# Delta-rule attention and a low-rank mixer: channel products placed one instruction at a time

## Chip, cores and metric

The kernel runs on one core of a Trainium2 chip. Times are device microseconds of one execution on that core. The kernel before took 682.71 us, the median of 13 runs between 678.31 and 686.07.

## What is computed

All data is fp32. There are 4 batches of 8 heads, 768 tokens and head dimension 48; the heads side by side make 384 channels, and the mixer's inner width is 1536. Cut to what matters:

```python
# attention: a 48x48 state per batch and head, token after token
k_n = k / (norm(k) + 1e-6)
for t in range(S):
    y[t]  = q[t] @ state
    state = state + beta[t] * outer(k_n[t], v[t] - k_n[t] @ state)
# bridge: (B, H, S, D) -> x of shape (B, S, H*D)
h  = x.transpose(0, 2, 1) @ U @ V          # mixes tokens, rank 32
u  = x + h.transpose(0, 2, 1)
out = u + relu(u @ w_ch1) @ w_ch2          # the two channel products
```

## The kernel before, in words

**Attention** works in chunks of 64 tokens, 12 to a batch, and in halves of 6 chunks, numbered n = 0 to 7 (two to a batch). For each half the keys, queries and values are loaded (`load_keys`, `load`, `load_queries`), the keys' norms and gates are made (`norms`), and `grams` turns keys and queries on TensorE (`turn`, line 506) and forms their small products (`products`, line 520), two chunks at a time, so three pairs for keys and three for queries. `blocks` inverts the 32-token triangular blocks on VectorE, by 31 pairs of operations (lines 651 and 657), moves them through a scratch in DRAM, and joins them on TensorE (lines 705 and 719). `recur` (line 849) then goes through the 12 chunks in order. A chunk is: a product with the state (`from_state`, line 853), a subtraction on VectorE (line 883, tile rhs), a product (line 890), a copy on ScalarE (line 899, tile z), two more sets of products (lines 904 and 912), the new state on VectorE (line 927), and two copies of the output to the token tile on ScalarE (line 934). All its matmuls are small, with 48 or 64 rows and 64 columns of the array.

**The mixer** works on half a batch, 384 tokens, at a time. `front` (line 941) makes the low-rank token mixing (lines 954 and 968), adds it on VectorE, and turns the result (line 976). `wide` (line 987) makes the two channel products. The first, lines 1004 to 1016, goes over 12 slices f of the inner width; each slice is three matmuls 128x128 by 384 into one PSUM tile p_f, then a relu on ScalarE into h_f. The second, lines 1020 to 1037, goes over three blocks of 128 tokens; each accumulates 12 matmuls into a tile p_o, which VectorE adds to x and SyncE stores. Over the whole kernel these are 288 matmuls of each kind.

**The order of the work** is written by a small planner in the kernel itself, lines 104 to 179, before anything runs; the chip's engines then follow the written order. Each of the functions above is a Python generator. It yields `need(...)`, a list of results that must have been written, and `step(...)`, which says what the instructions up to the next yield cost on each engine in estimated microseconds, which PSUM tiles they take and give back, and how long afterwards (`then`) the next step can start. `run` (line 138) keeps an estimated clock for each engine. It picks again and again the step that could start earliest; on a tie, the part with the lower place comes first. Places are given at lines 1041 to 1056: recurrences of batches 1 to 3 have 5.01 to 5.03, grams from 2.1 to 5.5, `front` 1.5, `relu`, `store` and the blocks of `front` 1, and `wide` 6 to 9.5. A part with a place under 5 that becomes ready within 0.4 of a chosen step's own time on the same engine goes ahead of it (lines 160 to 165). Batches meet in three places: `front` needs the recurrence of its own batch, `recur(b)` needs batch b - 2 to be mixed (line 863), and the loads of a half need the recurrence of an earlier one.

PSUM is shared by tags, each with two slots: "pair" (two banks each) for the recurrence and later grams, "one" for turns, norms and `front`, "mix" for the channel products, early grams and early joins. A step that takes a tag is not picked while the planner counts no free slot of it.

The step that matters here, in the first channel product, covers three matmuls at an estimated 1.95 us:

```python
            yield step(pe=1.95, take=("mix",))
            p_f = ps_mix([128, GT], "p_f")
            for t in range(KT):
                nc.tensor.matmul(
```

Of the kernel before, what the change touches and what calls it, by code (L numbers as in the profile page):

```python
# [19 lines left out]
GT = 384  # L20
# [5 lines left out]
def kernel(  # L26
# [31 lines left out]
    DM = H * D  # L58
# [16 lines left out]
    mix = ctx.enter_context(tc.tile_pool(name="mix", bufs=2))  # L75
# [7 lines left out]
    def ps_pair(name):  # L83

        t = psum.tile([128, 2, 512], FP32, name=name, tag="pair", bufs=2)
        return t

    def ps_tile(shape, name, tag):
        t = psum.tile([128, 512], FP32, name=name, tag=tag, bufs=2)
        dims = "abcd"[: len(shape) - 1]  # L90
        return t[0 : shape[0], 0 : math.prod(shape[1:])].rearrange(
            f"p ({' '.join(dims)}) -> p {' '.join(dims)}", **dict(zip(dims, shape[1:]))
        )

    def ps_one(shape, name):
        return ps_tile(shape, name, "one")

    def ps_mix(shape, name):
        return ps_tile(shape, name, "mix")
# [9 lines left out]
    def need(*keys):  # L109

        return [k for k in keys if all(x >= 0 for x in k[1:])]

    def step(pe=0, dve=0, act=0, sp=0, pool=0, then=0.0, on=None, take=(), give=()):

        return dict(
            pe=pe, dve=dve, act=act, sp=sp, pool=pool, then=then, on=on, take=take, give=give
        )

    def emitted(key, after=0.0):
        done[key] = clock["now"] + after
# [9 lines left out]
    def begin(part, place):  # L132

        i = (place, len(parts))
        parts[i], waits[i] = part, []
        advance(i, clock["now"])
# [130 lines left out]
    def w1_there(f):  # L267
        return "weights", 1 + KT * (f * 128 // WIDE + 1)

    def w2_there(f):  # L270
        return "weights", 2 + KT * DFF // WIDE + f // 2
# [74 lines left out]
    def half(i, size=L):  # L346
        return slice(L * i, L * i + size)
# [151 lines left out]
    def grams(n, place):  # L499


        yield need(("k", n), ("room", n), ("pg", 0 if n == 1 else -1))
        kn = keys[n]
        kq, pg, qk = made[n]

        def turn(ts, places):

            p_t = ps_one([128, 2, 2, 2 * L], "p_t")
            yield step(pe=0.45, then=0.1, take=("one",))
            for x, (t, c) in enumerate(ts):  # L510
                for j in range(2):
                    nc.tensor.transpose(  # L512
                        p_t[:, x, j],
                        t[:, c, 2 * j : 2 * j + 2].rearrange("p s d -> p (s d)"),
                        ident,
                    )
            yield step(act=0.6, then=0.1, give=("one",))
            nc.scalar.copy(places, p_t)  # L518

        def products(c0, i):  # L520

            banks = ("mix", "mix") if n < 3 - i else ("pair",)
            yield step(pe=0.8, then=0.1, take=banks)
            if len(banks) == 2:
                p_g = [ps_mix([128, 512], "p_g") for _ in range(2)]
            else:
                t = ps_pair("p_g")
                p_g = [t[:, par] for par in range(2)]
            p_g = [t[:, 0:256].rearrange("p (c j t) -> p c j t", c=2, j=2) for t in p_g]
            for c in range(2):  # L530
                for j in range(2):
                    for par, x in QUADS:
                        rows, cols = half(par, D), half(x)

                        to = half(1 - x) if par == 1 and i == 0 else cols
                        nc.tensor.matmul(  # L536
                            p_g[par][to, c, j],
                            kq[rows, c0 + c, j, 0, cols],
                            kq[rows, c0 + c, j, i, cols],
                            start=True,  # L540
                            stop=True,
                        )
            at = slice(c0, c0 + 2)
            if i == 0:
                yield step(**{"dve" if n == 0 else "act": 0.7}, give=banks)
                copy = nc.vector.tensor_copy if n == 0 else nc.scalar.copy
                for par in range(2):
                    copy(pg[:, at, par], p_g[par])
            else:
                yield step(dve=0.9, give=banks)  # L550
                for par in range(2):
                    nc.vector.tensor_tensor(  # L552
                        out=qk[:, at, par],
                        in0=p_g[par],
                        in1=mask_u[:, None, None, :].to_broadcast([128, 2, 2, L]),
                        op=ALU.mult,
                    )

        def key_pair(c0):
            if n > 2 and c0 + 2 > UC // 2:  # L560
                yield need(("ksq", n))
            yield from turn([(kn, c0), (kn, c0 + 1)], kq[:, c0 : c0 + 2, :, 0])
            emitted(("keys turned", n, c0 // 2))
            yield from products(c0, 0)
            emitted(("p", n, c0 // 2), 0.5)

        def query_pair(c0):
            yield need(("q", n), ("p", n, c0 // 2))
            yield from turn([(qt, c0), (qt, c0 + 1)], kq[:, c0 : c0 + 2, :, 1])
            yield from products(c0, 1)  # L570
            emitted(("g", n, c0 // 2), 0.5)

        qt = qns[n == 1]
        key_place, query_place = place
        for c0 in range(0, UC, 2):
            begin(key_pair(c0), key_place + 0.001 * c0)
        yield need(*[("p", n, i) for i in range(UC // 2)])
        emitted(("pg", n))
        for c0 in range(0, UC, 2):
            begin(query_pair(c0), query_place + 0.001 * c0)  # L580
        yield need(*[("g", n, i) for i in range(UC // 2)])
        emitted(("grams", n))
        emitted(("turned", n))
# [403 lines left out]
    def wide(b, i):  # L987
        yield need(("front", b, i), ("narrow", b - (i == 0), 1 - i))
        x, ut, hs = xs[b], uts[b, i], {}

        def relu(f, p_f):
            yield step(act=0.5, then=0.1, give=("mix",))
            hs[f] = mix.tile([128, GT], FP32, name="h_f", bufs=12)
            nc.scalar.activation(hs[f], p_f, ACTF.Relu)  # L994
            emitted(("h", b, i, f))

        def store(c, p_o):
            yield step(dve=0.57, sp=0.4, give=("mix",))
            nc.vector.tensor_tensor(out=x[:, c], in0=x[:, c], in1=p_o, op=ALU.add)  # L999
            nc.sync.dma_start(out=out[b, c * 128 : (c + 1) * 128, :], in_=x[:, c])  # L1000
            if c + 1 == NB:
                emitted(("mixed", b))

        for f in range(FT):
            yield need(w1_there(f))
            yield step(pe=1.95, take=("mix",))
            p_f = ps_mix([128, GT], "p_f")
            for t in range(KT):
                nc.tensor.matmul(  # L1009
                    p_f,  # L1010
                    w1_sb[:, t, f * 128 : (f + 1) * 128],
                    ut[:, t],
                    start=(t == 0),
                    stop=(t == KT - 1),
                )
            begin(relu(f, p_f), 1)
        emitted(("wide", b, i))
        first = i * GT // 128

        for cs in [(0, 1), (2,)] if (b, i) == (0, 0) else [(0,), (1,), (2,)]:  # L1020
            p_os = {}
            for f in range(0, FT, 3):
                for c in cs:
                    yield need(w2_there(f + 2), ("h", b, i, f + 2))
                    yield step(pe=1.95, take=("mix",) if f == 0 else ())
                    if f == 0:
                        p_os[c] = ps_mix([128, DM], "p_o")
                    for e in range(f, f + 3):
                        nc.tensor.matmul(  # L1029
                            p_os[c],  # L1030
                            hs[e][:, c * 128 : c * 128 + 128],
                            w2_sb[:, e],
                            start=(e == 0),
                            stop=(e == FT - 1),
                        )
            for c in cs:
                begin(store(first + c, p_os[c]), 1)
        emitted(("narrow", b, i))
# [16 lines left out]
    for b in range(B):  # L1055
        order += [(wide(b, 0), 6 + b), (wide(b, 1), 6.5 + b)]
# [35 lines left out]
```

## Time and profile before

| what | before |
|---|---|
| median of 13 runs | 682.71 us |
| profiled execution, own time | 680.38 us |
| its span | 678.7 us |
| TensorE matmul busy | 630.3 us, 93% |
| VectorE busy | 316.5 us, 47% |
| ScalarE busy | 200.7 us, 30% |
| GpSimd busy | 42.6 us, 6% |
| first channel product (line 1009) | 203.9 us, 576 records of 498 ns |
| second channel product (line 1029) | 200.8 us, 576 records of 495 ns |
| mean DMA rate | 68 GB/s |

A page of the profile tells of one execution. Busy times are the union of an engine's records. An fp32 matmul leaves two records. Matmuls are pipelined, so records overlap, and the distance from one start to the next says more than the length of a record. A group's line gives the source line, engine, operation, output and inputs, shape, count, busy time and mean length, then the idle time of the engine ahead of it and what ended most of that. The granted TensorE clock is 1.00 from 140 us to the end, apart from one stretch at 0.91 and the last at 0.97, and lower before that.

### The profile page before, as it was taken

How to read it: one execution, taken by the hardware profiler on the slowest of the kernel's cores; microseconds unless marked ns; L12 is line 12 of the kernel's file. 1: busy time of each engine (PE TensorE's matmuls, PEld its weight loads, DVE VectorE, ACT ScalarE, POOL GpSimd, SP SyncE). 2: the span in 40 equal slices, each digit the busy share in tenths (PEclk: the TensorE clock that was granted, in tenths of full speed). 3: DMA queues.
4: the chain of work that ended last, by engine and by line, in shares of the span. 5: the costliest groups of instructions: out<-in, count | busy, mean ns of one | idle time of the engine just before them, and what ended most of it. 6: DMA issues, size and time to landing. Idle time of an engine off the chain costs nothing.

```text
span 678.7 us, 19659 instructions
## 1 busy us (share of the span) xinstructions
PE 630.3 (93%) x8668; PEld 403.4 (59%) x8668; DVE 316.5 (47%) x791; ACT 200.7 (30%) x487; POOL 42.6 (6%) x80
## 2 busy tenths in 40 slices
PE   5538899689999999999999999999999999999997
PEld 4438788556555665566556654655655555555554
DVE  6666777888794228736812594377111011000000
ACT  2405566343411531243214323403221220120210
POOL 6451000100000000000000000000000000000000
PEclk9855755699999999998999999999999999999999
DMA  8586738736513322262033404110200000000000
GB/s 123 111 198 129 165 111 205 176 67 120 143 31 72 76 49 48 69 108 61 2 81 77 95 2 94 38 47 26 37 14 25 2 0 24 12 1 23 12 10 26
DMA packets 143892, 46.00 MB, mean 68 GB/s; under 512 B 136960, under 2 KB 140032, under 8 KB 143808
## 3 DMA queue, kind: packets, MB, share of 16 engines
q1 hardware_dynamic: 133952, 30.99, 22.8%
q0 software_dynamic: 3552, 12.88, 6.7%
q10 hardware_dynamic: 6304, 0.89, 0.8%
q8 instruction: 68, 1.11, 0.7%
q14 instruction: 16, 0.13, 0.1%
HBM read 33.62 MB, written 11.11 MB: 66 GB/s over the span
## 4 chain that ended last, share of the span: by engine, by line
PE 77%; DVE 10%; DMA 7%; ACT 2%; issue 2%; SPq 2%; ACTq 1%; DVEq 0%
PE p_f L1009 27%; PE p_o L1029 26%; PE p_g L536 4%; PE p_y L853 3%; PE p_t L512 3%; PE p_h L968 3%; DVE prod L651 2%; PE p_s L904 2%; DVE xt L657 2%; PE p_s L890 2%; DMA zt<-scr 2%; PE p_y L912 2%; DMA scr<-xt 1%; PE p_e L777 1%; PE p_u L976 1%
## 5 line engine op out<-in xcount | busy, mean ns | idle before, releaser
L1009 PE MATMUL p_f<-ut,w_sb 128*128 128x384 f32 x576 | 203.9, 498 | 0.2 <-ACT h_f L994 0.2
L1029 PE MATMUL p_o<-w_sb,h_f 128*128 128x384 f32 x576 | 200.8, 495 | 0.2 <-DVE x L999 0.2
L1029 PEld LDWEIGHTS p_o<-w_sb,h_f 128*128 128x128 f32 x576 | 104.8, 190 | 64.5 <-DVE x L999 0.4
L1009 PEld LDWEIGHTS p_f<-ut,w_sb 128*128 128x128 f32 x576 | 104.7, 191 | 63.9 <-issue 1.5
L994 ACT ACTIVATE h_f<-p_f 128x384 f32<-128x384 f32 x96 | 47.1, 491 | 200.9 <-PE p_f L1009 200.8
L657 DVE TENSOR_TENSOR xt<-xt,prod 96x112 f32<-96x112 f32 (+21 forms) x216 | 70.5, 326 | 7.4
L651 DVE TENSOR_TENSOR prod<-gs,xt 96x112 f32<-96x112 f32 (+21 forms) x216 | 70.0, 324 | 5.9
L999 DVE TENSOR_TENSOR x<-x,p_o 128x384 f32<-128x384 f32 x24 | 13.2, 552 | 125.4 <-PE p_o L1029 125.4
L536 PE MATMUL p_g<-kq 48*64 48x64 f32 x1536 | 41.0, 254 | 11.4 <-DVE qk L552 8.1
L927 DVE TENSOR_TENSOR s<-s,p_s 128x192 f32<-128x192 f32 x40 | 14.1, 352 | 69.7 <-PE p_s L904 68.6
L536 PEld LDWEIGHTS p_g<-kq 48*64 48x64 f32 x1536 | 34.7, 162 | 19.6 <-DVE qk L552 7.6
L934 ACT COPY x<-p_y 64x192 f32<-64x192 f32 x96 | 30.1, 314 | 47.6 <-PE p_y L912 41.9
L853 PEld LDWEIGHTS p_y<-s,kq 48*64 48x64 f32 x1408 | 28.7, 153 | 20.1 <-issue 12.9
L853 PE MATMUL p_y<-s,kq 48*64 48x48 f32 x1408 | 34.2, 241 | 1.4 <-DVE prod L651 1.1
L883 DVE TENSOR_TENSOR rhs<-vn,p_y 128x192 f32<-128x192 f32 x44 | 15.5, 353 | 42.7 <-PE p_y L853 42.3
L899 ACT COPY z<-p_s 128x192 f32<-128x192 f32 x48 | 15.3, 320 | 65.6 <-PE p_s L890 65.4
L518 ACT COPY kq<-p_t 128x512 f32<-128x512 f32 x48 | 27.4, 588 | 19.5 <-PE p_t L512 19.1
L890 PEld LDWEIGHTS p_s<-rhs,zt 64*64 64x64 f32 x704 | 16.3, 148 | 22.1 <-issue 17.9
L904 PEld LDWEIGHTS p_s<-z,kn 64*64 64x64 f32 x704 | 16.5, 151 | 20.6 <-issue 17.9
L552 DVE TENSOR_TENSOR qk<-p_g,mask_u 128x256 f32<-128x256 f32 x48 | 17.7, 414 | 16.7 <-PE p_g L536 16.4
L890 PE MATMUL p_s<-rhs,zt 64*64 64x48 f32 x704 | 21.8, 242 | 3.8 <-DVE qk L552 3.5
L972 DVE TENSOR_TENSOR x<-x,p_h 128x384 f32<-128x384 f32 x24 | 13.3, 554 | 24.6 <-PE p_h L968 23.9
(120 smaller groups left out, 525.7 us busy)
## 6 DMA issues: line engine op xcount, KB each, us to landing
wide<-in_moe_w_ch_dram POOLq DMA_DIRECT2D x6, 768.0 KB, 5.3
stage<-in_moe_w_ch_dram POOLq DMA_DIRECT2D x6, 768.0 KB, 5.2
out_dram<-x SPq DMA_DIRECT2D x24, 192.0 KB, 1.9
kn<-in_k_dram SPq DMA_DIRECT2D x60, 72.0 KB, 3.0
qn<-in_q_dram SPq DMA_DIRECT2D x48, 72.0 KB, 3.5
vn<-in_v_dram SPq DMA_DIRECT2D x48, 72.0 KB, 2.5
gs<-scr SPq DMA_DIRECT2D x8, 384.0 KB, 3.3
scr<-xt SPq DMA_DIRECT2D x8, 384.0 KB, 3.2
```

Of the source, the lines that this page charges most:

```text
L512: nc.tensor.transpose(p_t[:, x, j], t[:, c, 2 * j : 2 * j + 2].rearrange("p s d -> p (s d)"), ident,)
L518: nc.scalar.copy(places, p_t)
L536: nc.tensor.matmul(p_g[par][to, c, j], kq[rows, c0 + c, j, 0, cols], kq[rows, c0 + c, j, i, cols], start=True, stop=True,)
L651: nc.vector.tensor_tensor(out=prod, in0=gb[:, :, j : j + 1, j + 1 :].to_broadcast([NP, split, m, w]), in1=xb[:, :, 0:m, j : j + 1].to_broa ...
L657: nc.vector.tensor_tensor(out=xb[:, :, 0:m, j + 1 :], in0=xb[:, :, 0:m, j + 1 :], in1=prod, op=ALU.subtract,)
L853: nc.tensor.matmul(p[half(x ^ par), par, D * (2 * i + j) : D * (2 * i + j) + D], kq[half(par, D), cu, j, i, half(x)], s_old[half(par, D), ...
L890: nc.tensor.matmul(p_s[half(x), par, D * (2 + j) : D * (2 + j) + D], zt[half(x ^ par), cu, par, j], rhs[half(x ^ par), 2 * j + par], start ...
L904: nc.tensor.matmul(p_s[half(par), x, D * j : D * j + D], kn[half(x), cu, 2 * j + par], z[half(x), 2 * j + par], start=True, stop=True,)
L934: nc.scalar.copy(tokens_of(b, c, g), pair_of(p_y, 1)[half(g)])
L994: nc.scalar.activation(hs[f], p_f, ACTF.Relu)
L1009: nc.tensor.matmul(p_f, w1_sb[:, t, f * 128 : (f + 1) * 128], ut[:, t], start=(t == 0), stop=(t == KT - 1),)
L1029: nc.tensor.matmul(p_os[c], hs[e][:, c * 128 : c * 128 + 128], w2_sb[:, e], start=(e == 0), stop=(e == FT - 1),)
```

## The change

The estimated cost of the channel products was given for three matmuls together, in one step. Now each matmul is a step of its own, at 0.65 us, so that the planner can put steps of attention between any two of them. The PSUM tile is taken with the first. The tile in `turn` is now named after its step's yield. Nothing else is touched: the same instructions are written, in another order.

```diff
         def turn(ts, places):
 
+            yield step(pe=0.45, then=0.1, take=("one",))
             p_t = ps_one([128, 2, 2, 2 * L], "p_t")
-            yield step(pe=0.45, then=0.1, take=("one",))
...
         for f in range(FT):
             yield need(w1_there(f))
-            yield step(pe=1.95, take=("mix",))
-            p_f = ps_mix([128, GT], "p_f")
             for t in range(KT):
+                yield step(pe=0.65, take=("mix",) if t == 0 else ())
+                if t == 0:
+                    p_f = ps_mix([128, GT], "p_f")
                 nc.tensor.matmul(
...
                     yield need(w2_there(f + 2), ("h", b, i, f + 2))
-                    yield step(pe=1.95, take=("mix",) if f == 0 else ())
-                    if f == 0:
-                        p_os[c] = ps_mix([128, DM], "p_o")
                     for e in range(f, f + 3):
+                        yield step(pe=0.65, take=("mix",) if e == 0 else ())
+                        if e == 0:
+                            p_os[c] = ps_mix([128, DM], "p_o")
                         nc.tensor.matmul(
```

## The prediction, made before the change was run

> **What bounds the kernel now.** I read the engine totals first, then a table by stage, then what TensorE waited for, then the timeline inside a stage. From the page, engines and groups of instructions:
>
> ```profile
> PE 630.3 (93%) x8668; PEld 403.4 (59%) x8668; DVE 316.5 (47%) x791; ACT 200.7 (30%) x487; POOL 42.6 (6%) x80
> ...
> L1009 PE MATMUL p_f<-ut,w_sb 128*128 128x384 f32 x576 | 203.9, 498 | 0.2 <-ACT h_f L994 0.2
> L1029 PE MATMUL p_o<-w_sb,h_f 128*128 128x384 f32 x576 | 200.8, 495 | 0.2 <-DVE x L999 0.2
> ```
>
> TensorE leads, and two lines, the mixer's two channel products, fill 405 us of it. Each is 288 matmuls; the trace shows 576 records, two passes a matmul. The table by stage:
>
> ```profile
> 0.00:146.00 146.00, 107.71 (x2429) 90.70 (x2430) 106.98 (x250) 61.84 (x160) 35.55 (x72) 0.67 0.69 149
> ...
> 183.00:284.00 101.00, 100.76 (x1535) 61.06 (x1534) 59.01 (x166) 27.98 (x70) 0.98 (x1) 1.00 0.25 54
> 284.00:313.00 29.00, 26.68 (x477) 16.69 (x476) 12.08 (x25) 11.99 (x29) 0.98 (x1) 0.95 0.62 122
> ...
> 567.00:679.00 112.00, 108.25 (x336) 63.46 (x334) 4.59 (x9) 12.19 (x25) 0.00 (x0) 1.00 0.04 16
> ```
>
> Columns are stretch, length, then busy us of PE, weight load, DVE, ACT, POOL. Before 146 us there is no mixer product, so the edit reaches nothing there. From 183 us TensorE is full: 100.76 of 101 us while the recurrence of batch 1 runs, and mixer alone after 567. Only the stretches between recurrences leak (26.68 of 29). What TensorE waited for from 146 us on (total, times, longest):
>
> ```profile
> PE p_g L536 <- issue: 1.5, 1, 1.5
> PE p_v L719 <- issue: 1.3, 1, 1.3
> PE p_u L976 <- DVE x L972: 0.6, 1, 0.6
> ```
>
> These are TensorE's largest waits after 146 us; the whole list of 11 sums to 5.8 us, and the two largest wait for no engine. A sum over the stages agrees: 533 us less busy time is 10.4 us, of which 3.7 lies after the last matmul. So at most some 6 us of visible idleness can be won. The timeline of batch 1's recurrence (start, length, engine and operation):
>
> ```profile
> 193.04 0.45 PE L890 MATMUL p_s<-rhs,zt 64*64 64x48 f32 x16
> ...
> 193.42 2.20 PE L1029 MATMUL p_o<-w_sb,h_f 128*128 128x384 f32 x6
> 193.56 0.32 ACT L899 COPY z<-p_s 128x192 f32<-128x192 f32 x1 [4.61 <-PE p_s L890]
> ...
> 195.55 0.45 PE L904 MATMUL p_s<-z,kn 64*64 64x48 f32 x16
> ...
> 195.82 0.41 PE L912 MATMUL p_y<-z,qk 64*64 64x48 f32 x16
> ...
> 196.17 2.20 PE L1029 MATMUL p_o<-w_sb,h_f 128*128 128x384 f32 x6
> ...
> 198.30 0.68 PE L853 MATMUL p_y<-s,kq 48*64 48x48 f32 x32
> ```
>
> This is the pattern of a recurrence: a small step, a block of three channel products (six records), a small step. I call each stretch of channel products between small ones a visit. Counting visits in this timeline gives 123: 6 in 146 to 183 us, 34, 34 and 33 in the three recurrences, 4 and 6 between them, 6 after 546.
>
> **Where busy time hides a cost.** The last chain shows what streaming costs:
>
> ```profile
> 652.03 23.23 PE p_o L1029 x72
> ```
>
> 23.23 / 72 = 0.323 us a record, 0.645 a matmul, so three stream in 1.94 us. In the recurrence the visit at 193.42 holds the engine until 195.55, 2.13 us: 0.20 us is lost in entering and leaving. The small side loses too:
>
> ```profile
> 243.47 0.68 PE L853 MATMUL p_y<-s,kq 48*64 48x48 f32 x32
> 243.97 0.66 PE L536 MATMUL p_g<-kq 48*64 48x64 f32 x32
> ```
>
> Here p_y before another small step takes 0.50 us to the next start; at 198.30, before a channel product (198.91), 0.61. So a visit costs 0.20 us to 0.31; I take 0.27. All 123 cost some 33 us.
>
> **What the Trainium skill says.** "TensorEngine Tiling (Array Packing)", Key Properties: changing the tiling mode "drains the TensorE". The small steps use 64*64 or 48*64 tiles and the products 128*128; the trace agrees, with the 0.20 us above. "Perfetto Trace Analysis", Identifying the Most-Contended Engine: matmul busy share is a poor measure of the distance to peak. It agrees here: the 0.20 us counts as busy. "TensorE: Matmul & The Clock Gate", Part 3, The mechanism: matmuls start and end in program order. So a small step that waits holds the products written behind it; I found no record out of order.
>
> **The change part by part.**
>
> The tile of `turn` is named after its yield. Nothing is added; the planner counts slots by `take`, not by names. In the old order three turns are named at once although the tag has two slots, so a name can't claim a slot. I take 0; any effect would lie before 146 us, and I bound it at 1 us either way.
>
> The matmuls are unchanged in number: 2 x 288 x 0.645 = 372 us before and after. No DMA, copy or wait is added as such; relu and store still follow the last product of their tile.
>
> The split moves attention earlier. After each small step the planner places the channel product, which can start at once, then returns to the recurrence (its place, 5.0x, goes before the mixer's 6 and up on a tie). By its own figures the recurrence is back 0.27 to 0.47 us after TensorE is free, so one product of 0.65 covers it where three stood. A chunk has three gaps; its small steps take 0.61 + 0.38 + 0.27 + 0.34 = 1.60 us from start to start (193 to 199 us). With three visits of 2.13 us a chunk is 8.0 us; with three single ones (0.645 + 0.20 = 0.845) it is 4.1. A recurrence of 12 chunks shrinks from about 98 us to 50. This wins nothing by itself: the products left over run later, in long visits, on the same full engine. A recurrence also waits for the batch two before it to be mixed, so attention can't run far ahead, and the mixer never lacks work.
>
> What counts is visits. In a recurrence each gap still needs one: some 101, as before. Between recurrences more appear. There the old schedule ran out of channel products (batch 0's last was at 282 us, when the recurrence ended) and placed 29 small steps (13 of `front`, 16 of grams and blocks) with 4 and 6 visits. Now products are left over, and a single one fits each gap of 0.5 to 0.7 us behind an ACT or DVE copy; if two small steps go between visits, 29 steps make 14. That is 8 to 10 more, twice. In 146 to 183 us I guess 6 to become 12; after 546, 6 to become 8. Part of the grams no longer fits into the shorter recurrence and adds about 3, twice. Sum: 18 + 6 + 2 + 6 = about 32; I take 30, from -10 to 60. 30 x 0.27 = +8 us.
>
> Against this, leftover products fill idle time between recurrences: of 6 us I take 3, since the two waits on issue (2.8) have no engine to wait for.
>
> New waits: the cover of a gap falls from 2.13 us to 0.85. From the timeline, z is ready at 193.88, 0.46 us after TensorE is free at 193.42. In the same way rhs and s take a DVE operation of 0.35 us plus about 0.1: all under 0.85. While DVE inverts blocks, its pairs (0.42 + 0.42) stand ahead: s ended at 197.61, 1.44 us after TensorE was free. The planner knows of these pairs (0.84 for the longest) and would place two products (1.49). It also takes a lone product for 0.65 where it really lasts 0.85, so TensorE runs later than planned and its helpers are early. I take 0 for new waits; the other end is a rival below.
>
> Queues: loads of keys, queries and values (eight DMAs, 5 to 6 us of SP issue each) and the scratch round trips of the blocks are issued earlier relative to the stores; POOL's xt clear moves with them. SP issues little (DMA share 0.25 and less inside recurrences), and products lie behind any late landing. I take 0.
>
> Sum: +8 - 3 + 0 = +5 us. The profiled execution took 680.38 us (span 678.7 and 1.7 around it); 685.4 against it. The median of the 13 runs is 682.71, 0.3% higher; I put the same +5 on it: 687.5.
>
> **Rivals.**
>
> A, gaps filled, no more visits (faster, -4 us, 678.5). If small steps join up between recurrences as they do now, visits stay near 123 or fall, and most idle time, 3 to 6 us, is filled. For it: 10.4 us of idleness exists, mostly where products had run out. Against: a finer filler offers more places to switch. Chance 0.25.
>
> B, the split moves work and no more (682.7). Visits and idle time cancel, or a gap still takes three in a row because attention is held by the blocks' DMAs. Chance 0.15.
>
> C, my forecast, more visits (+3 to +12, 687.5). Chance 0.47.
>
> D, one product doesn't cover a gap (slower, 703). TensorE runs in written order; if a DVE pair stands ahead and only one product was placed, it waits 1.44 - 0.85 = 0.6 us. It decides from a delay of 0.85 us on. About a third of 101 gaps at 0.6 give +20 us. Against: the planner's DVE figures are not below the real ones. Chance 0.13.
>
> **How the numbers follow.** About 0.3%, 2 us, is what a measurement of this kernel can tell from no change. A gives faster by more: 0.25. B gives within: 0.15. C and D give slower: 0.60. The range reaches from inside A (678) to between C and D (699), leaving about 0.2 outside. Faster and slower both hold much; C's own range is 685 to 695.
>
> **What would show it.** Right: the first mixer product still at 146 us; recurrence stretches of 50 to 60 us with two-record visits in the gaps; small lists of waits; 140 to 170 visits; a mixer-only tail of over 200 us in place of 111. A shows as under 125 visits and less idle time. D shows as PE waits on rhs, s or z in the recurrences, summing to over 10 us. I am wrong if the visit's 0.20 us shrinks for a lone product, or if the planner keeps blocks together.

## The result, and the profile after

The changed kernel took 690.53 us, the median of 11 runs between 687.55 and 694.69, against 682.75 us for the kernel before. The ratio is 1.0109 with a 95% interval of 1.0087 to 1.0132: slower by some 7.5 us, where +5 was forecast. Medians here are of all executions, and ratios leave out those more than 1.5% above the fastest of the same kernel (three of `again`, two of `second_only`). The profiled execution took 693.09 us, its span 691.4. It lies near the upper end of the runs, so waits found in it have to be looked for in a second profile as well. The page of the kernel after, engines and groups:

```profile
PE 633.4 (92%) x8668; PEld 398.6 (58%) x8668; DVE 316.8 (46%) x791; ACT 201.0 (29%) x487; POOL 42.6 (6%) x80
...
L1010 PE MATMUL p_f<-ut,w_sb 128*128 128x384 f32 x576 | 217.0, 512 | 3.4 <-issue 3.2
```

The number of instructions is as before. The first channel product is 13 us busier, 512 ns a record where it was 498, and has a wait of 3.2 us in front of it. The table by stage of the kernel after (stretch, length, then busy us of PE, weight load, DVE, ACT, POOL, granted clock, DMA share, GB/s):

```profile
0.00:146.00 146.00, 103.03 (x2426) 85.53 (x2427) 106.10 (x249) 61.33 (x159) 35.54 (x72) 0.65 0.69 149
146.00:183.00 37.00, 32.88 (x452) 20.50 (x451) 29.27 (x62) 16.36 (x33) 3.17 (x4) 0.94 0.49 109
183.00:285.00 102.00, 98.75 (x1503) 57.81 (x1506) 58.80 (x162) 27.41 (x70) 0.98 (x1) 0.95 0.24 51
...
467.00:516.00 49.00, 49.00 (x987) 27.49 (x986) 8.36 (x23) 17.60 (x47) 0.00 (x0) 1.00 0.02 7
516.00:691.00 175.00, 171.75 (x548) 99.83 (x548) 10.54 (x19) 21.67 (x45) 0.00 (x0) 1.00 0.04 14
```

Four things are to be seen. The first 146 us hold the same work. The last recurrence, 467 to 516 us, has shrunk to 49 us, and TensorE is busy in all of it. What was left over stands at the end: attention is done at 516, so nearly all of the last 175 us is mixer. And the stage from 183 us, where TensorE had been busy 100.76 of 101 us before, is now 98.75 of 102 at a clock of 0.95. What TensorE waited for from 146 us on, in the kernel after (total, times, longest):

```profile
PE p_f L1010 <- issue: 3.2, 1, 3.2
PE p_v L719 <- issue: 3.2, 3, 1.4
PE p_y L853 <- DVE s L927: 3.0, 1, 3.0
```

In the kernel before, the longest was 1.5 us and the whole list 5.8. Here two single waits of some 3 us lead it, and the list sums to 10.9. One of them has an engine behind it, DVE with the state s, inside a recurrence. The timeline inside the last recurrence of the kernel after shows what the change was meant to do (start, length):

```profile
470.71 0.91 PE L1010 MATMUL p_f<-ut,w_sb 128*128 128x384 f32 x2
471.56 0.68 PE L853 MATMUL p_y<-s,kq 48*64 48x48 f32 x32
472.17 0.91 PE L1010 MATMUL p_f<-ut,w_sb 128*128 128x384 f32 x2
473.01 0.45 PE L890 MATMUL p_s<-rhs,zt 64*64 64x48 f32 x16
...
474.84 0.91 PE L1010 MATMUL p_f<-ut,w_sb 128*128 128x384 f32 x2
```

Two records, one product, stand in each gap. A chunk takes 474.84 - 470.71 = 4.13 us, and a visit 471.56 - 470.71 = 0.85 us, which is the 0.645 of its stream and 0.20. No step waits.

**A ledger.** From the start times I split the time between the first channel product and the end of the last one. The stream is 1152 records at 0.3225 us, 371.5 us in every kernel. A visit costs what it usually loses in entering and leaving, which turned out to depend on its neighbours: 0.197 us between two steps on tiles under 128x128, 0.10 where one neighbour is a step on 128x128 tiles (`front`'s lines 968 and 976, `turn`), nothing between two such. A small step costs its usual time from start to start. What goes more than 0.15 us over the usual is called a wait, the slow clock after it included.

| us | before | after | after, second profile |
|---|---|---|---|
| first product at | 146.5 | 145.7 | 144.4 |
| from it to the end of the last | 528.6 | 542.0 | 531.6 |
| visits (number) | 21.0 (123) | 25.0 (166) | 25.0 (166) |
| small steps | 124.1 | 121.8 | 121.8 |
| waits | 8.8 | 20.7 | 10.2 |
| rest | 3.2 | 3.0 | 3.1 |

The second profile is of the run called `again` below, an execution of 681.27 us, which is at the lower end of that kernel's times. The two profiles bracket the median. The first product is written five records earlier after the change, so the first row does not compare the same point. Visits and small steps cost the same in both: +4.0 and -2.3, together +1.7 us. Waits are +1.4 in one and +12 in the other. So of the +7.5 us at the median some 2 are visits less cheaper small steps, and the rest, some 6, I put down to waits. That share is a remainder and not a measurement: no profile is of an execution at the median, and the one of the kernel before lies 2.3 us under its own.

**The wait inside the recurrence.** The chain of waits of the kernel after, in the window from 252 us (start, length, what):

```profile
251.49 3.40 DMA gs<-scr
...
254.91 1.23 DVE gs L635
...
256.24 0.20 DVE prod L651
...
257.07 0.35 DVE s L927
...
257.56 1.11 PE p_y L853 x32
```

Read backwards: TensorE's p_y needs the state s. VectorE had not been busy with other work, it stood at line 635, waiting for gs, and s is written behind it in VectorE's order. gs is the read of the blocks (line 618) from DRAM, which SyncE issued at 251.49. Why so late, SyncE's timeline of the kernel after shows:

```profile
244.01 7.43 SPq L371 DMA_DIRECT2D qn<-in_q_dram  x8
251.49 0.61 SPq L618 DMA_DIRECT2D gs<-scr  x1
```

Eight loads of queries were written ahead of it and took SyncE 7.43 us to issue; the planner reckons two groups at 2.6, 5.2 us in all. In the kernel before the same two, the read of half 4 and the queries of half 5, stood the other way round:

```profile
250.21 0.31 SPq L618 DMA_DIRECT2D gs<-scr  x1
...
264.03 5.28 SPq L371 DMA_DIRECT2D qn<-in_q_dram  x8
```

and VectorE reached its use of gs without a wait:

```profile
253.21 1.22 DVE L635 TENSOR_TENSOR gs<-gs,cp 96x1024 f32<-96x1024 f32 x1
```

There too this half is read during the recurrence of batch 1, at almost the same time. With single products the queries' turn comes earlier, the eight loads (at 264 us before, 244 after) step in front of the read, and VectorE's wait for its DMA (4.14 us in the trace) now holds the state of another batch. Two products were the cover. The clock then makes it dearer (windows of the kernel after, granted clock in the third column from the end):

```profile
175.34:178.75 3.41, 1.54 (x97) 1.09 (x97) 1.82 (x3) 2.26 (x4) 0.00 (x0) 1.00 1.01 279
178.76:185.58 6.82, 4.99 (x8) 2.86 (x9) 3.91 (x5) 1.35 (x3) 0.77 (x1) 0.50 0.30 65
253.85:257.26 3.41, 0.67 (x3) 0.05 (x1) 2.14 (x6) 0.00 (x0) 0.00 (x0) 1.00 0.08 22
257.27:264.08 6.81, 6.52 (x70) 3.60 (x74) 3.87 (x14) 0.81 (x2) 0.00 (x0) 0.50 0.01 2
424.51:427.92 3.41, 1.75 (x99) 1.41 (x99) 2.03 (x5) 0.25 (x1) 0.00 (x0) 1.00 0.04 11
427.93:431.34 3.41, 3.41 (x7) 1.75 (x6) 3.06 (x11) 1.97 (x3) 0.00 (x0) 0.50 0.02 5
```

Around the wait that ended at 180.59, after the one that ended at 257.56, and after a shorter one at 427 us, TensorE runs at half clock: busy and getting half as much done. "TensorE: Matmul & The Clock Gate", Part 1, The HAM clock gate, in the Trainium skill tells of a clock that halves after an idle window of about 3.4 us. The half agrees; TensorE was not idle for a whole window here, the waits being 3.2, 3.0 and 1.4 us.

The clock records of the traces show how such a wait counts. In each profile all changes of the clock lie whole multiples of 3.41 us apart, and the stretches at 0.50 after the first product are one or two such periods long. In the fourteen profiles of this document, after the first product, each of the 13 periods at full clock in which TensorE was busy 51% or less (45, 20 and 51% above) was followed by half clock; of the seven with 53 to 60%, two were; of those with more, one (68%, in `before_gs_late`). So what counts is how a wait falls into these periods, and they lie differently in each execution. After the first product the profile above spent 17.1 us at half clock, the one of the kernel before 3.4.

### The profile page after: what moved, and what is told of

Read it like the earlier page. It is cut to its first block, busy times and chain, and to the rows that moved or that the text cites. A ratio compares the mean times of both kernels' runs of the same rounds, so it can differ in the third digit from the quotient of the medians.

```text
span 691.4 us, 19658 instructions
## 1 busy us (share of the span) xinstructions
PE 633.4 (92%) x8668; PEld 398.6 (58%) x8668; DVE 316.8 (46%) x791; ACT 201.0 (29%) x487; POOL 42.6 (6%) x80
## 4 chain that ended last, share of the span: by engine, by line
PE 76%; DVE 8%; DMA 7%; ACT 3%; issue 3%; SPq 2%; ACTq 0%; DVEq 0%
PE p_o L1030 28%; PE p_f L1010 25%; PE p_y L853 3%; PE p_g L536 3%; PE p_h L968 3%; PE p_s L890 2%; PE p_s L904 2%; PE p_t L512 2%; PE p_u L976 2%; PE p_y L912 2%; DMA scr<-xt 1%; PE p_e L777 1%; DMA gs<-scr 1%; DMA kn<-in_k_dram 1%; DVE prod L651 1%
## 5 line engine op out<-in xcount | busy, mean ns | idle before, releaser
L1010 PE MATMUL p_f<-ut,w_sb 128*128 128x384 f32 x576 | 217.0, 512 | 3.4 <-issue 3.2
L1030 PE MATMUL p_o<-w_sb,h_f 128*128 128x384 f32 x576 | 203.2, 495 | 0.0
L536 PE MATMUL p_g<-kq 48*64 48x64 f32 x1536 | 37.7, 243 | 10.3 <-DVE qk L552 8.2
L536 PEld LDWEIGHTS p_g<-kq 48*64 48x64 f32 x1536 | 31.8, 153 | 23.0 <-ACT kq L518 8.7
```

Of the source, the lines that this page charges most:

```text
L536: nc.tensor.matmul(p_g[par][to, c, j], kq[rows, c0 + c, j, 0, cols], kq[rows, c0 + c, j, i, cols], start=True, stop=True,)
L1010: nc.tensor.matmul(p_f, w1_sb[:, t, f * 128 : (f + 1) * 128], ut[:, t], start=(t == 0), stop=(t == KT - 1),)
L1030: nc.tensor.matmul(p_os[c], hs[e][:, c * 128 : c * 128 + 128], w2_sb[:, e], start=(e == 0), stop=(e == FT - 1),)
```

## The experiments

My theory: the edit does two things. It adds visits, which cost a few us, and it moves the written order, so that a wait enters which isn't there before, above all the one on gs for half 4 (the third batch's first half, read at 251 us). The rival: the added visits are the loss, and the waits are chance of one execution. Where an expectation has another rival, it names it.

### The changed kernel again, and each half of the change

`again` is the changed kernel unaltered. `first_only` and `second_only` are the kernel before with the split in the first or in the second channel product alone:

```diff
-            yield step(pe=1.95, take=("mix",))
...
             for t in range(KT):
+                yield step(pe=0.65, take=("mix",) if t == 0 else ())
```

> The changed kernel once more, for a second profile. My theory: of the 7.5 us, some are changes between the products' 128*128 tiles and the small steps' tiles (166 visits of channel products in place of 123, of which 114 in place of 97 stand between small-tile steps on both sides, at 0.20 us each), some are new waits that the written order makes: the state's VectorE operation (line 927) written behind one that waits for the blocks' read from DRAM (line 635), and the half clock that follows. It expects a ratio of 1.009 to 1.013, and TensorE waiting 2 to 4 us on the state once more at about 255 us. The rival, that these waits are a chance of one execution and visits alone count, expects the same ratio, but no such wait in this profile.

> The kernel before, with only the first channel product placed one matmul at a time. 147 visits, 108 of them between small-tile steps on both sides (before 123 and 97; changed kernel 166 and 114). If visits alone make the loss, it lies between the two in proportion: 24/43 of 7.5, +4 us, ratio 1.006. If waits of the written order count as much, it can be anywhere from 0.998 to 1.012, and the profile's list of TensorE waits must tell which.

> The kernel before, with only the second channel product placed one matmul at a time. 147 visits, 108 between small-tile steps, the same as with the first product alone. Visits alone: the same time as that kernel, ratio 1.006. Waits of the written order: a different time from that kernel by 2 us or more, with the difference in TensorE's waits.

| kernel | median (runs), us | ratio to before | visits |
|---|---|---|---|
| again | 689.56 (15) | 1.0080, 1.0055 to 1.0105 | 166 |
| first_only | 686.16 (7) | 1.0060, 1.0035 to 1.0085 | 147 |
| second_only | 685.45 (22) | 1.0028, 1.0008 to 1.0049 | 147 |

Both halves are slower than before, and the sum of their parts, 0.60 + 0.28%, is about the whole. `again` came out just under its range of 1.009 to 1.013. `first_only` is at the 1.006 that visits alone would give, and `second_only`, with as many visits, below it; but their intervals overlap, so this pair decides nothing. TensorE's waits in `again`, from 140 us on:

```profile
PE p_y L853 <- DVE s L927: 2.5, 1, 2.5
PE p_v L719 <- issue: 2.4, 3, 1.2
PE p_f L1010 <- issue: 1.2, 1, 1.2
```

The wait on s is there again, so it belongs to the program. `second_only` has it too, 3.3 us, with the same eight loads ahead of the read; that its median is only 0.3% above the kernel before speaks against a high price of this one wait. The wait of p_f on issue is the one at 177 us; it is 1.2 us here and 3.2 in the other execution. And no halved clock followed in this one. The two clock periods of `again` on which the wait on s fell, and the window behind it:

```profile
246.12:249.53 3.41, 2.26 (x37) 1.24 (x36) 1.22 (x2) 1.12 (x3) 0.00 (x0) 1.00 0.29 99
249.53:252.95 3.42, 2.10 (x37) 1.27 (x37) 3.11 (x14) 0.49 (x1) 0.00 (x0) 1.00 0.00 0
251.00:257.00 6.00, 6.00 (x123) 3.62 (x120) 5.59 (x19) 1.92 (x5) 0.00 (x0) 1.00 0.01 3
```

The wait is half a microsecond shorter and lies across the border of two periods, busy 66 and 61%. In the 6 us behind it 123 records ran at a clock of 1.00; in the other execution 70 ran in 6.8 us at 0.50. The 10.5 us between the ledger's waits of the two profiles come from this: some 3 us are more waiting (from 146 us on, lists of 10.9 and 7.6), and some 7.5 are half clock, which is half of the 14.9 us that TensorE was busy at 0.50.

**What stands behind "issue".** No engine releases the wait at 177 us, but the trace's DMA packets show what came just ahead of its end. The page of the kernel after lists them in sum:

```profile
q8 instruction: 68, 1.11, 0.7%
```

These are 68 packets of 16 KB with instructions, for TensorE's 17336 matmuls and weight loads 255 to a packet. In the kernel after one landed at 179.36 us and the wait ended at 180.59; in `again` one landed at 175.88 and the wait ended at 177.23. In the fourteen profiles there are 34 waits of TensorE on "issue" over 0.6 us after 140 us, and 33 of them ended 1.2 to 1.6 us after such a landing. So TensorE seems to have waited for its own instructions, mostly at or just behind blocks like p_x and p_v, which take 96 matmuls and 96 weight loads in 1.0 us. This is read off the times alone; no run changed it. Why one fetch began 1.0 us ahead of the wait and the other 0.6 after its start is open.

### What a visit costs, by itself

To the kernel before, 288 small matmuls (64*64 tiles, 48 columns, into an unused PSUM tile) are added, among the 72 products of the last half batch: four after each product in `tail_72x4`, twelve after every third in `tail_24x12`. They are the same matmuls in number; only the visits differ, 72 against 24.

```diff
+            if count[0] % 1 == 0:
+                for _ in range(4 * 1):
+                    nc.tensor.matmul(
+                        extra[0][0:64, 0, 0:D], zts[0][0:64, 0, 0, 0], kns[1][0:64, 0, 0, 0:D],
+                        start=True, stop=True,
+                    )
```

(In `tail_24x12` both ones are threes.)

> Measures a visit's price alone. The kernel before, with 288 extra small matmuls (64*64 tiles, 48 columns, into an unused PSUM tile) in the last half batch, where the mixer runs alone: four after each of its 72 channel products. From the traces a small block of eight records takes about 0.26 us and a visit loses 0.20: 72 x 0.46 = +33 us, ratio 1.048. If visits are free (the loss is made up by the stream): 72 x 8 x 0.015 = +8 us, ratio 1.012.

> The same 288 extra small matmuls, twelve after every third product, so 24 visits in place of 72. With the visit's price: 24 x (0.49 + 0.20) = +17 us, ratio 1.024, 16 us less than with 72 visits, or 0.34 us for a visit, both sides. If visits are free: the same as with 72, +8 us, ratio 1.012.

Measured: 737.85 us (6 runs, 1.0806, 1.0771 to 1.0841) and 725.23 us (6 runs, 1.0615, 1.0579 to 1.0651). Both missed their expectations (1.048 and 1.024), since the small matmuls cost more than was taken for them; their difference is what was wanted. It is 12.6 us over 48 visits, 0.26 us a visit, both sides together, where 0.34 was expected. The timelines of `tail_72x4`,

```profile
690.13 0.66 PE L1012 MATMUL p_z<-kn,zt 64*64 64x48 f32 x8
690.73 0.91 PE L1046 MATMUL p_o<-w_sb,h_f 128*128 128x384 f32 x2
691.57 0.66 PE L1012 MATMUL p_z<-kn,zt 64*64 64x48 f32 x8
```

and of `tail_24x12`,

```profile
689.06 2.20 PE L1046 MATMUL p_o<-w_sb,h_f 128*128 128x384 f32 x6
691.20 1.59 PE L1012 MATMUL p_z<-kn,zt 64*64 64x48 f32 x24
692.72 2.20 PE L1046 MATMUL p_o<-w_sb,h_f 128*128 128x384 f32 x6
```

show it directly. A visit of one product holds TensorE 691.57 - 690.73 = 0.84 us, 0.20 above its 0.645; one of three holds it 691.20 - 689.06 = 2.14, 0.20 above its 1.935. The loss doesn't depend on the number of products. The forecast's price, 0.27 us, stands for visits between small tiles. What it does not say is how many of the new visits are of that kind. Both kernels took far longer than the 24 or 72 visits explain: a small record costs (692.72 - 691.20) / 24 = 0.063 us here, the visit's other side included, where in the recurrence 16 take 0.38 us. Here all are the same matmul in one place of the array, there they alternate between places; that this is the reason was not tested.

In the changed kernel, visits between 128x128 steps lose nothing. Its timeline at 291 us, inside `front`:

```profile
290.89 0.55 PE L976 MATMUL p_u<-ident,x 128*128 128x128 f32 x3
291.27 0.81 PE L1030 MATMUL p_o<-w_sb,h_f 128*128 128x384 f32 x2
291.92 0.49 PE L976 MATMUL p_u<-ident,x 128*128 128x128 f32 x3
```

291.92 - 291.27 = 0.65 us, the bare stream. By the tiles of both neighbours in the traces, of the visits before (the first and the last left out) 100 lay between smaller tiles, 17 had a 128x128 step on one side and 4 on both; after, it is 115, 29 and 20, where four beside a step on 128x24 tiles count as beside a full one, since they lost 0.03 us or less. (The expectations' 97 and 114 leave out a few beside steps on 128x32 tiles, which lost as much as the others.) So 15 new ones at 0.197, 12 at 0.10 and 16 for nothing: 3.0 + 1.2 = 4.2 us, near the ledger's 4.0.

### Taking away the wait on the blocks' read

The step that reads the blocks gives the time to its landing as `then`. A longer estimate makes the planner put VectorE's use of gs later. `gs_late` does so for halves 2 to 7, `gs_late_4` for half 4 alone, and `before_gs_late` makes the edit of `gs_late` on the kernel before.

```diff
-        yield step(sp=0.4, pool=0.9 if n > 1 else 0, on="sp", then=3.2)
+        yield step(sp=0.4, pool=0.9 if n > 1 else 0, on="sp", then=3.2 if n < 2 else 7.0)
```

(`gs_late_4`: `then=7.0 if n == 4 else 3.2`.)

> The changed kernel, but the planner is told that the blocks' read from DRAM takes 7.0 us instead of 3.2 for halves from 2 on, so that VectorE's first operation on it is written later and the recurrence's state isn't queued behind a wait. 162 visits, 112 between small-tile steps. My theory: the wait of 3 us on the state and the half clock after it go, 4 to 6 us less than the changed kernel, ratio to before 1.003 to 1.006. The rival, visits alone: 4 visits fewer, less than 1 us, ratio 1.010.

> The changed kernel, with the longer estimate (7.0 us) of the blocks' read from DRAM for half 4 alone, the half whose read made VectorE and then TensorE wait. 166 visits as in the changed kernel, 115 between small-tile steps. My theory, that this one wait and the half clock after it are most of the loss: ratio to before 0.997 to 1.002, some 7 us less than the changed kernel. The rival, that the gain of the kernel with all halves late came from several places (or from the order as a whole): less than half of that gain, ratio 1.004 to 1.009.

> The kernel before with the longer estimate for halves from 2 on; three matmuls at a time. 123 visits as before, 100 between small-tile steps in place of 97. My theory: its VectorE waits cost TensorE nothing, since three products cover them; ratio 0.998 to 1.002. The rival, that the longer estimate is good by itself whatever the size of a step: ratio 0.990 to 0.996.

| kernel | median (runs), us | ratio to before | visits | ledger: visits, small steps, waits |
|---|---|---|---|---|
| gs_late | 681.00 (22) | 0.9978, 0.9964 to 0.9991 | 162 | 24.7, 122.7, 9.4 |
| gs_late_4 | 684.25 (22) | 1.0004, 0.9984 to 1.0024 | 166 | 25.1, 122.4, 7.9 |
| before_gs_late | 686.04 (22) | 1.0049, 1.0033 to 1.0066 | 123 | 21.2, 124.7, 15.6 |

`gs_late` gained more than was expected of it (1.003 to 1.006). In `gs_late_4` one number, the estimate for one half, brings the changed kernel from 1.0109 (1.0080 in `again`) back to 1.0004, with the same 166 visits. That speaks against the rival: the visits stayed and the loss went. What TensorE waits for in `gs_late_4`:

```profile
PE p_f L1010 <- issue: 2.2, 1, 2.2
PE p_v L719 <- issue: 1.2, 2, 1.0
```

The wait on s is gone; that of p_f at 177 us stays. This profile fell on the fastest execution, 678.81 us, and has no half clock after the first product. But `before_gs_late` was a miss for theory and rival alike. The kernel before has no such wait, and the same edit made it slower by 3 us. The head of its list of waits shows what came in:

```profile
PE p_v L719 <- ACT xz L714: 2.3, 1, 2.3
```

The edit rewrote the order, and with it came this wait of 2.3 us, with a stretch at half clock behind it, and at 314 us a second such stretch; the ledger's waits are 15.6 against 8.8. So any edit of an estimate shuffles which waits there are, and `gs_late` alone doesn't prove that this one wait was the loss. It needs a kernel that takes the same wait away without touching an estimate.

### The same wait, by order; and singles only in recurrences

`read_first` leaves the estimates and makes the queries of half 5 wait, in the planner's order, for the blocks' read of half 4 to be written:

```diff
-        yield need(("turned", n - 1), ("turned", 0))
+        yield need(("turned", n - 1), ("turned", 0), ("read", 4 if n == 5 else -1))
...
         nc.sync.dma_start(out=gs[:, 0:BK], in_=scr)
+        emitted(("read", n))
```

> The changed kernel, with the queries of half 5 written behind the blocks' read of half 4 on SyncE's queue, where they had stood ahead of it. Nothing else is asked for, though the planner's later choices follow. 158 visits, 111 between small-tile steps (changed kernel 166, 114). My theory: the read lands some 7 us earlier, VectorE doesn't wait for it with the state behind, and the time falls as it did with the longer estimate for half 4: ratio to before 0.997 to 1.003. The rival, that the longer estimate helped by a better order in general and not by the wait: ratio 1.006 to 1.011.

Measured: 687.91 us (16 runs), 1.0066 (1.0045 to 1.0087), with 158 visits: the rival's range. The edit did what it should. SyncE's timeline of `read_first`,

```profile
239.59 0.47 SPq L618 DMA_DIRECT2D gs<-scr  x1
240.16 5.77 SPq L371 DMA_DIRECT2D qn<-in_q_dram  x8
```

has the read first, and the wait on s is gone from TensorE's list:

```profile
PE p_f L1011 <- issue: 2.2, 1, 2.2
...
PE p_s L891 <- issue: 1.6, 1, 1.6
PE p_s L891 <- DVE prod L652: 1.2, 1, 1.2
```

But two others of 1.6 and 1.2 us stand in recurrences in its place, and the ledger's waits are 12.5. Both are waits for rhs on VectorE. In the first, rhs was written from 249.11 to 249.45 behind pairs of a block inversion, and the matmul started at 249.55. In the second it was written at 365.79 behind line 636, which had itself waited 2.27 us for the blocks' read of another half. Taking away the one wait by its cause won about 2 us (687.91 against 689.56 and 690.53), not the 6 that `gs_late_4` won. The theory in its narrow form, one wait, falls. What stays is that the written order as a whole now carries waits.

`recur_only_late` has `gs_late`'s estimate and splits the products only while a recurrence is under way; elsewhere three stay together.

```diff
-                yield step(pe=0.65, take=("mix",) if t == 0 else ())
+                if live or t == 0:
+                    yield step(pe=0.65 * (1 if live else KT), take=("mix",) if t == 0 else ())
```

> The changed kernel with the longer estimate of the blocks' read, and single products only while a recurrence is under way, three at a time elsewhere. 148 visits, 110 between small-tile steps, against 162 and 112 with the longer estimate alone (ratio 0.998). By the visit's price, 0.20 to 0.26 us for those between small-tile steps and little for those beside full-tile steps, fewer visits are worth under 1.5 us: ratio 0.995 to 0.999. The rival, that every visit costs 0.26: 14 fewer, -3.6 us, ratio 0.993. Above 1.002 would mean that a wait of the written order has come back.

Measured: 688.44 us (6 runs), 1.0082 (1.0051 to 1.0112), 148 visits. Fewer visits than `gs_late` and 7 us slower. Its waits:

```profile
PE p_v L719 <- ACT xz L714: 3.0, 2, 2.5
```

The wait of p_v on a ScalarE copy, 2.5 us with half clock behind it, is the kind that `before_gs_late` had: a wait of the written order came back, which is what "above 1.002" was to mean. The time does not follow the visits. That these waits make all of the 7 us is not shown.

### The estimate of SyncE's loads, with and without the split

If the order is at fault, the fault should lie in what the planner believes. It reckons 2.6 us for four loads; the traces show 7.43, 6.47 and 5.77 us for eight, 2.7 to 3.7 for four. Both kernels get 3.4 from the third half on, in `fetch`:

```diff
-                yield step(**{names[queue]: 2.6})
+                yield step(**{names[queue]: 2.6 if n < 2 else 3.4})
```

> The changed kernel, with the planner told 3.4 us in place of 2.6 for four of SyncE's fetch DMAs from half 2 on, nearer to the traces (2.7 to 3.7). 157 visits, 112 between small-tile steps. My theory: a truer estimate of the queue lets the planner write VectorE's operation later or the read earlier, so the wait on the state is under 1 us; ratio 0.996 to 1.004. The rival, that only the two edits made by hand hit that wait: ratio 1.006 or more, with TensorE waiting on the state in the profile.

> The kernel before, three products at a time, with the same truer estimate of SyncE's fetches (3.4 us). Against single products with that estimate (ratio 0.995) it tells whether the split or the estimate makes that kernel the fastest so far. My theory, that three products hide such waits and the estimate changes little here: ratio 0.998 to 1.003, so the split with a truer estimate is worth 0.3 to 0.8%. The rival, that the estimate alone is the gain: ratio 0.992 to 0.997.

| kernel | median (runs), us | ratio to before | visits | ledger: visits, small steps, waits |
|---|---|---|---|---|
| sp_34 (single products) | 679.51 (7) | 0.9946, 0.9927 to 0.9965 | 157 | 24.2, 121.8, 9.1 |
| before_sp_34 (three together) | 679.10 (22) | 0.9937, 0.9918 to 0.9956 | 125 | 21.5, 123.5, 7.7 |

With the estimate nearer to the traces both are faster than either kernel of the study, and they are equal: `sp_34` below the range of its theory, `before_sp_34` in that of the rival. The longest of TensorE's waits in `sp_34`,

```profile
PE p_v L719 <- ACT xz L714: 1.4, 1, 1.4
PE p_v L719 <- issue: 1.1, 2, 0.7
```

and in `before_sp_34`,

```profile
PE p_v L719 <- issue: 2.7, 2, 2.1
```

are short. The split by itself is then worth nothing that these runs can tell: visits 2.7 us dearer, small steps 1.7 cheaper, waits 1.4 more. The gain came with the estimate and not with the split, since the kernel before has it as well. Why it came is not shown. The profile of `before_sp_34`, of an execution at its upper end (681.71 us), has a ledger only 1.2 us below that of the kernel before, and one value was tried: a lucky order is not excluded.

## Why the forecast was right, point by point

**The sign and most of the size held, for half the reason given.** Forecast +5, measured +7.5. In the forecast +8 came from visits, -3 from filled gaps and nothing from waits; on the chip visits cost +4.0, small steps -2.3, and some 6 are left for waits and the half clock behind them. That the sum came near is luck: visits were put too high by about as much as the waits were left out.

**Visits: count and price right, sum too large.** "140 to 170 visits", about 153, were forecast, and there are 166. The price of 0.27 us was confirmed at 0.26 by the pair of tail kernels, and it doesn't shrink for a lone product. But "30 x 0.27 = +8 us" put that price on every new visit. Most of the new ones were forecast between recurrences, where nearly half of the small steps are `front`'s; its steps at lines 968 and 976 are 128x128 like the products, and between two such a visit is free. 43 new visits cost +4.0. "TensorEngine Tiling (Array Packing)", Key Properties, which I had cited for the drain at a change of tiling mode, already says by its wording that there is none where the mode stays; I had not looked at the tiles of both neighbours.

**Filled gaps: in part.** Of 6 us of idleness 3 were taken as won. Without the two waits on s and p_f the lists sum to 4.7 and 3.9 us in the two profiles, against 5.8 before: 1 to 2 us were won. The ledger's 2.3 us on small steps are another thing, their usual time from start to start, and were not forecast.

**Chunks and recurrences: right for the last recurrence, wrong for the two before it.** 4.1 us a chunk and 50 us a recurrence were forecast; the last recurrence has 4.13 and 49. The ones of batches 1 and 2, with VectorE inverting blocks beside them, took some 92 and 81 us, because the planner put two products in many gaps. The lengths are 104 single, 45 double and 6 triple among the visits of whole products, where before 117 were triple. The mixer-only tail was forecast at over 200 us and is 175.

**`turn`: taken at nothing.** TensorE's order up to the first channel product is the same in both traces, apart from independent matmuls that start within a few hundredths of a microsecond. The first product stands at 144.4 and 145.7 us in two profiles of the kernel after, and between 143.9 and 148.8 in all the profiles, whatever the edit. No kernel with that line alone was run.

**Queues and new waits: the step that failed.** "SP issues little ... and products lie behind any late landing. I take 0", and "I take 0 for new waits". Neither holds. What lay behind a late landing was not a product on TensorE but the state's update on VectorE. The blocks' read came behind eight loads that SyncE takes 7.43 us to issue, VectorE stood 4.14 us for it, and TensorE 3.0. I had counted queues by how busy they are; what counts is which instruction stands in front of which. The waits on "issue" grew as well, from 2.8 us in sum to 6.4 and 3.6, and had no term. Nor was there a term for the clock, which stood at 0.50 for 17.1 us in one profile and not at all in the other. The cost of new waits with it is +1.4 us in one profile and +12 in the other; some 6 are left for it at the median.

**The rivals.** A, gaps filled with no more visits, is out: 166 visits and slower. B is out for the kernel as changed, but `sp_34` and `before_sp_34` are as B has it: equal times. D had a part of the mechanism, VectorE's queue ahead of the state, but not its place or its price: not a third of the gaps at 0.6 us, but one gap, at 3.0 us, with a DMA at the head of the queue, and a halved clock after it. In `read_first` a wait of D's own kind does appear, rhs behind VectorE's pairs, but once and at 1.6 us.

**Open.** The price of the wait on s is not settled: `gs_late_4` puts it at 5 to 6 us, `read_first` at 2, and both move other work. That the waits marked "issue" are waits for instructions rests on their times alone. Nor is it settled what halves the clock after a period between half and two thirds busy.

## What to carry to other kernels

On a full engine, splitting the filler work finer cost little here by the switches of tile that it added, +4 us; count them by both neighbours. The gain was as small, since the work is the same. The risk lies in the cover: where a step hides behind 0.85 us in place of 2.1, a late DMA at the head of another engine's queue shows at once, so what stands in which order in each queue has to be read rather than how busy it is. Where an order is planned from estimates, compare those with the trace first, and try each correction on the kernel before as well: here the gain came with a corrected estimate, with the split and without it.

## What the hardware showed that I had not expected

- A visit of 128x128 products loses 0.197 us between steps on smaller tiles, 0.10 with one 128x128 neighbour, and nothing between 128x128 steps.
- A wait of 1.4 to 3.2 us inside dense work can be followed by one or two periods of 3.41 us at a clock of 0.50: from 180.59 us nine records took 5.46 us from start to start, 0.61 each in place of 0.3225. It followed each of the 13 periods in which TensorE was busy 51% or less; a wait of 2.5 us that fell across two periods was not followed by it.
- Of 34 waits of TensorE that no engine releases, 33 ended 1.2 to 1.6 us after a 16 KB packet of instructions had landed.
- One and the same program took from 681.27 to 694.69 us, and the profiles at 681.27 and 693.09 us differ by 10.5 us of waits, some 7.5 of them half clock.
- The same small matmul repeated in one place of the array cost some 0.06 us a record; those of the recurrence, which alternate between places, take 0.38 us for 16.
